# A refitted planner, a reordered opening and seven-product down matmuls from an earlier chunk, in a fused AFNO and GEGLU kernel

## The chip, the cores and the metric

The kernel runs on one core of one Trainium2 chip. Its time is the device time of one execution in microseconds (us); what counts is the median over the runs. The core has five engines that run side by side, each with its own queue in order: PE (TensorE, matmuls; its weight loads are listed as PEld), DVE (VectorE), ACT (ScalarE), POOL (GpSimd) and SP (SyncE, which here issues nearly all DMAs).

## The reference

A token-wise layer norm feeds two branches. Branch s is a Fourier transform over 8192 positions, a two-layer complex block MLP on the frequencies with a soft threshold, and the inverse transform. Branch g is a gated feed-forward network with 1792 hidden units. The output is the input plus their product.

```python
N, D, F = 8192, 448, 1792          # positions, channels, hidden units
xn = layernorm(x)
s = A(xn)      # rfft2 -> (x @ w1 + b1, relu) -> (@ w2 + b2) -> soft threshold 0.01 -> irfft2, 4 blocks of 112
g = silu((gelu(xn @ w_gate) * (xn @ w_up)) @ w_down)
out = x + s * g
```

All operands are float32. The kernel splits each into a high and a low float16 half, and makes one product from three matmuls: high with high, high with low, low with high.

## The kernel before

**The feed-forward network.** Positions are cut into 16 chunks of 512 tokens. The 14 slices of 128 hidden units are worked in two passes over all chunks: pass 0 has 8 slices, pass 1 has 6. A pass-0 result is stored to DRAM (`prt`) and fetched again in pass 1. Chunks 0 and 1 of pass 0 are computed plainly (`plain`, in `ffn`), while the weights still arrive. From chunk 2 on the up and gate products use Winograd's form of Strassen's scheme, seven products in place of eight (`unit`, with pairs of slices and halves of the tokens), on token factors that DMA transposes bring from DRAM (`xts` to `xta` and `xtb`).

**The down product of a chunk** has two forms. `down` makes 3 matmuls of 448 columns for each of 4 token tiles and each slice. `down2` uses seven products too: for each pair of slices 7 products, 2 halves and 3 matmuls of 224 columns, and once a 64-column filler. It needs sums of the hidden values (`sums` within `unit`; their halves go into the tiles `h`, `left` and, in pass 1, `wt`), and it adds the products up with `add2`, on ACT for the first part of a result and on DVE for the others. It also leaves a part of its work, the "tail", to be run inside the next chunk.

**The factored down weights.** `weights` first makes the combinations of the 8 near weight slices (`gu_comb`), then four times `factor0`, which fetches a pair of rows of the down weights, forms their seven factors and writes them to DRAM (`dsp`). When the fourth has been written, plus 3 us, `state["products"]` is set. `chunk` looks at it when it begins: at the first chunk that finds the flag and meets a condition on its number, it sets `seven` for good and starts `factors_in(0)`, 26 loads on SP that bring the factors into `dw`, `wt` and `left`.

**The other work.** Phase 1 runs beside the feed-forward network: `chunk1` normalises a chunk, writes its token factors (`xts`) and does the first stage of the transform, whose matmuls are called `bd<-xs,m`. `begin` does this for chunk 0 (`begin1` for chunk 1) together with the first weight slice; this is the opening. Phase 2 is the block MLP on the frequencies, phase 3 the inverse transform (`tiles3`) and the output.

**The order is planned when the program is built.** `Pace` is a small simulator of time. Every operation goes through `Engine`, whose call at L235 is the line of nearly every instruction in the profile. `Pace.start` asks when its engine and its operands are free, `Pace.cost` says how long it takes, and `Pace.issue` notes the end. The work is written as generators; whichever is due next in simulated time issues its instruction next, so the order of each engine's queue comes from the model. Side work asks with `calm`, which holds it back while its engine is busy or other work is due soon; `Either` gives an operation to whichever of two engines ends it first. The constants: `STEPS` gives corrections by stretch of time, `SLACK` a waiting time for PSUM banks, `T1` and `DT` the start of chunk 2's phase-1 work and the distance of the following ones, `END2` and `END3` the times over which the work of phases 2 and 3 is spread. The planner's times decide the order alone; on the chip the engines wait for one another with semaphores.

**The opening's weights.** `gu_loads` fetches the near slices 0 to 7 (`in_gu`, 512 KB each) into a ring `wst` of three slots, each large enough for a slice in its later form (`in_raw`, 17 columns of 128). `gu_block` and `gu_split` scale them into `wt`. Before the first matmul that counts, `keep` runs matmuls on ones.

Of the kernel before, what the change touches and what calls it, by code (L numbers as in the profile page):

```python
# [22 lines left out]
NG = 16  # L23
# [3 lines left out]
SLACK = 1.0  # L27
# [15 lines left out]
STEPS = ((0, 2.75, 0.05, 1), (100, 2.5, 0.15, 1.05), (175, 3, 0.2, 0.98), (250, 2.75, 0.05, 1), (325, 2.5, 0.05, 1), (400, 3.0, 0.1, 1.04), (475, 2.5, 0.05, 1), (550, 3.5, 0.05, 1), (700, 3.25, 0.3, 1), (775, 3.0, 0.3, 0.995), (850, 2.75, 0.05, 0.96), (925, 2.75, 0.05, 1.06), (1150, 2.5, 0.15, 0.995), (1450, 3, 0.1, 0.99), (1525, 2.75, 0.05, 1.02))  # L43
# [6 lines left out]
class Event:  # L50
    def __init__(self):
        self.done, self.waiting = False, []


class Pace:
# [4 lines left out]
    def __init__(self):  # L60
# [4 lines left out]
        self.late = False  # L65

# [72 lines left out]
    def ready(self, ap, write, engine):  # L139
        name, lo, hi = self.region(ap)  # L140
        return max((t + 0.12 for a, b, w, t, e in self.seen.get(name, ())
# [9 lines left out]
    def quiet(self, ap):  # L151
        return max((x[3] for x in self.seen.get(ap.tensor.name, ())), default=0.0)

    def start(self, e, out, ins):
        outs = [out] if out.space != bass.MemoryType.DRAM else []
        ins = [i for i in ins if i.space != bass.MemoryType.DRAM]
        return outs, ins, max([self.now, self.free.get(e, 0.0)] + [self.ready(i, False, e) for i in ins]
                              + [self.ready(o, True, e) for o in outs])

    def issue(self, e, op, out, ins, run):  # L160
        outs, ins, start = self.start(e, out, ins)
        if e == "SP" or op == "dma_start":
            size = (outs or ins)[0].nbytes()
            self.dma = max(self.dma, start) + size / (320e3 if start > 10.0 else 400e3)
            if start < 10.0:
                self.free[e] = start + 0.46
                end = self.dma + 0.9
            elif op == "dma_start_transpose":
                self.free[e] = start + 1.15 + size / 380e3
                end = max(self.free[e] + 2.6, self.dma + 1.5)  # L170
            else:
                self.free[e] = start + 0.5
                end = max(start + 2.2 + size / 240e3, self.dma + 1.5) + (self.step(start)[1] if outs and start > 100.0 else 0.0)
        else:
            end = start + self.cost(e, op, start, out, ins) * (1.0 if e == "PE" else self.step(start)[3])
# [2584 lines left out]
```

## Time and profile before

| | us |
|---|---|
| median of 3 runs (1759.02 to 1761.61) | 1759.36 |
| the profiled execution, own time | 1758.21 |
| its span, first to last instruction | 1756.4 |
| mean granted TensorE clock | 0.993 |

DMA moved 316.62 MB at a mean of 180 GB/s. The largest issues by count and size are the stores of token factors (`xts<-sx`, 32 of 480 KB), the loads of x and the raw weights (`wst<-in_raw`, 14 of 1088 KB). The factor loads appear as `dw<-dsp`, `wt<-dsp` and `left<-dsp`, the factor stores as `dsp<-wo`.

How to read the lines: a group is named out<-in by the program's tiles, with partitions x elements and type, then count, busy time and mean duration of one, then the idle time of the engine just before and what ended it. In a timeline a line has start, length, engine and operation; "x12" means that 12 alike were merged, and the bracket gives the idle time before it and who released it. PSUM banks are `bx`, `by` and `bd`. Matmul ends are modelled and matmuls overlap, so the price of one is read from the length of an unbroken run over its count.

### The profile page before, as it was taken

Reading aid. Unit: us, or ns where it says so; the run is one execution under the profiler, and the core shown is the slowest. Engines: PE = TensorE matmul, PEld = TensorE weight load, DVE = VectorE, ACT = ScalarE, POOL = GpSimd, SP = SyncE. Lnnn points to the kernel's source line nnn. Section 1 sums busy time; section 2 is a strip of 40 time slices with the busy share of each in tenths; the row PEclk is TensorE's granted clock in tenths of the full one; section 3 lists DMA queues with packets and bytes.
Section 4 is the critical chain, followed back from the end, with each engine's and each line's share of the span. In section 5 each row is a group of like instructions: output and inputs, shape, how many; then the busy total and the mean of one; then the engine's idle time right before and its main releaser. Section 6 shows DMA issues by size and latency. Waiting matters only on the chain.

```text
span 1756.4 us, 40962 instructions
## 1 busy us (share of the span) xinstructions
PE 1715.7 (98%) x15645; PEld 1435.9 (82%) x15645; DVE 1418.7 (81%) x2606; ACT 1113.9 (63%) x2279; POOL 751.5 (43%) x1083
## 2 busy tenths in 40 slices
PE   8998999999999999999999999999999999999997
PEld 4445677777777998999999989999899989889886
DVE  7898797777778877788887778888888887787787
ACT  6566676576676566778777666777676666333333
POOL 2277675566554564344333344432233432222222
PEclk9999999999999999999999999999999999999999
DMA  6428888887678653253445775445555545999996
GB/s 212 146 83 277 247 258 267 227 249 206 195 246 232 168 124 83 60 121 93 107 110 180 191 171 123 119 109 133 136 131 139 132 100 131 302 292 301 274 311 224
DMA packets 438308, 316.62 MB, mean 180 GB/s; under 512 B 305792, under 2 KB 409600, under 8 KB 436320
## 3 DMA queue, kind: packets, MB, share of 16 engines
q1 hardware_dynamic: 437824, 313.99, 63.6%
q8 instruction: 122, 2.00, 0.5%
q14 instruction: 74, 0.61, 0.1%
q10 hardware_dynamic: 288, 0.03, 0.0%
HBM read 137.93 MB, written 108.25 MB: 140 GB/s over the span
## 4 chain that ended last, share of the span: by engine, by line
PE 84%; DVE 7%; DMA 3%; ACT 3%; issue 2%; SPq 1%; POOL 1%; DVEq 0%; ACTq 0%; POOLq 0%
PE bd L235 34%; PE bx L235 29%; PE by L235 21%; DVE wt L235 1%; DVE u L235 1%; SPq L235 1%; DVE h L235 1%; DMA wst<-in_gu 1%; DMA prt<-th 1%; DVE va L235 1%; DMA xtb<-xts 1%; ACT h L235 1%; DVE o L235 0%; DMA vt<-va 0%; ACT o L235 0%
## 5 line engine op out<-in xcount | busy, mean ns | idle before, releaser
L235 PEld LDWEIGHTS <-wt 128*128 128x128 f16 x9142 | 887.2, 98 | 173.8 <-issue 19.4
L235 PE MATMUL bx<-xta,wt 128*128 128x256 f16 (+1 forms) x2819 | 355.5, 276 | 3.5 <-DMA xta<-xts 2.5
L235 PEld LDWEIGHTS <-h 128*128 128x128 f16 x2711 | 258.8, 98 | 73.5 <-DVE h L235 1.5
L235 PE MATMUL by<-xtb,wt 128*128 128x256 f16 x2080 | 255.7, 273 | 2.4 <-DVE by L235 1.3
L235 PE MATMUL bd<-dw,h 128*128 128x448 f16 (+1 forms) x1536 | 243.2, 306 | 0.0
L235 PE MATMUL bx<-xtb,wt 128*128 128x256 f16 x1248 | 153.2, 273 | 2.4 <-DVE v L235 2.3
L235 POOL TENSOR_TENSOR wt<-wt 128x256 f32<-128x256 f32 x81 | 63.0, 778 | 209.8 <-DVE wt L235 198.7
L235 PE MATMUL by<-xta,wt 128*128 128x256 f16 (+1 forms) x899 | 126.4, 285 | 2.7 <-ACT wt L235 1.9
L235 DVE TENSOR_TENSOR by<-bx,u 128x512 f32<-128x512 f32 x104 | 72.3, 695 | 43.4 <-PE bx L235 36.3
L235 ACT ACTIVATE u<-by,fc 128x512 f32<-128x512 f32 (+1 forms) x118 | 73.5, 635 | 47.9 <-PE by L235 47.0
L235 PE MATMUL bd<-dw,wt 128*128 128x224 f16 (+1 forms) x816 | 98.2, 264 | 3.6 <-DVE left L235 3.2
L235 PE MATMUL bx<-left,wt 128*128 128x256 f16 x816 | 100.0, 273 | 0.3 <-ACT by L235 0.3
L235 ACT COPY u<-by 128x512 f32<-128x512 f32 x104 | 60.7, 583 | 51.0 <-PE by L235 50.4
L235 ACT CAST h<-wt 128x512 f16<-128x512 f32 (+1 forms) x128 | 68.5, 536 | 36.1 <-DVE wt L235 29.1
L235 DVE TENSOR_TENSOR v<-bx,u 128x512 f32<-128x512 f32 x104 | 71.1, 684 | 16.1 <-PE bx L235 15.2
L235 DVE SCALAR_TENSOR_TENSOR left<-bd,ms,left 128x448 f32<-128x448 f32 x96 | 64.2, 678 | 22.5 <-PE bd L235 22.0
L235 ACT COPY by<-bx 128x512 f32<-128x512 f32 x104 | 60.1, 578 | 32.9 <-PE bx L235 32.6
L235 POOL TENSOR_TENSOR t<-h 112x256 f32<-112x256 f32 (+1 forms) x36 | 30.0, 832 | 114.3 <-ACT h L235 93.1
L235 PE MATMUL bd<-w2t,wn 113*128 113x112 f16 (+1 forms) x1152 | 78.1, 212 | 0.7 <-DVE wn L235 0.3
L235 PE MATMUL bd<-wt,h 128*128 128x224 f16 x603 | 72.2, 259 | 0.8 <-DVE h L235 0.7
L235 DVE SCALAR_TENSOR_TENSOR u<-by,fc,u 128x512 f32<-128x512 f32 (+1 forms) x86 | 55.4, 658 | 21.5 <-PE by L235 11.9
L235 PEld LDWEIGHTS <-wn 113*128 113x128 f16 (+1 forms) x1152 | 69.1, 97 | 3.8 <-POOL wn L235 0.6
(275 smaller groups left out, 3707.9 us busy)
## 6 DMA issues: line engine op xcount, KB each, us to landing
xts<-sx SPq DMA_DIRECT2D x32, 480.0 KB, 4.1
x<-in_x SPq DMA_DIRECT2D x17, 896.0 KB, 6.6
wst<-in_raw SPq DMA_DIRECT2D x14, 1088.0 KB, 7.0
t<-ysb SPq DMA_DIRECT2D x64, 224.0 KB, 3.5
prt<-th SPq DMA_DIRECT2D x64, 224.0 KB, 3.3
vt<-va SPq DMA_DIRECT2D x256, 56.0 KB, 2.1
left<-prt SPq DMA_DIRECT2D x64, 224.0 KB, 3.8
u<-t SPq DMA_DIRECT2D x32, 448.0 KB, 5.7
```

The source lines that it names most:

```text
L235: return self.pace.issue(self.name, kind, out, ins, lambda: fn(out, *args, **kw))
```

## The change

The change has three parts.

1. The planner's model is refitted. A result is seen by another engine after a delay that depends on the producer (`LATE`) instead of 0.12 us; an engine is free a little before its operation ends (`OVER`); any access to a PSUM bank waits for all others to it; DMAs get new rates, eight lanes and a lower rate for short runs; the costs of POOL and DVE are new; `SLACK`, `STEPS`, `T1`, `DT`, `END2` and `END3` get other values. No operation is added by this; the queues' order follows from it.
2. The opening is reordered. The near weight slices go into half-slots, six at a time instead of three; slices 6 and 7 wait until 0 and 1 have been read, and a whole slot is handed on for raw weights when both of its halves have been read. The number of matmuls on ones goes from 13 to 22. The maximum of the first weight slice is taken in two halves, and the normalisation and the casts of two token tiles stand between them. One low half moves from DVE to POOL and two go to DVE or POOL, whichever is planned to end first; the second copy of transposed tokens moves from ACT to DVE.
3. `chunk` asks for `i >= 2` instead of `i >= 9` before it goes over to seven down products.

The diff, cut to its core:

```diff
-SLACK = 1.0
+SLACK = 0.8
-STEPS = (...)
+STEPS = (...)
+LATE = {"PE": 0.2, "ACT": 0.04, "DVE": 0.04, "POOL": 0.05, "SP": 0.05}
+OVER = {"PE": 0.0, "ACT": 0.075, "DVE": 0.06, "POOL": 0.02}
...
     def ready(self, ap, write, engine):
         name, lo, hi = self.region(ap)
-        return max((t + 0.12 for a, b, w, t, e in self.seen.get(name, ())
+        write = write or ap.space == PSUM
+        return max((t + LATE[e] for a, b, w, t, e in self.seen.get(name, ())
                     if (write or w) and e != engine and a < hi and lo < b), default=0.0)
...
+            else:
+                turned = op == "dma_start_transpose"
+                slow = turned or min(self.run_of(a) for a in (out, ins[0])) < 512
+                self.dma = max(self.dma, start) + size / (210e3 if slow else 330e3)
+                self.free[e] = start + (1.0 + size / 305e3 if turned else 0.55)
+                end = max(self.dma + 1.7, self.free[e] + 2.6 * turned)
+            self.lanes = self.lanes[-7:] + [end]
         else:
+            n = start + self.cost(e, op, start, out, sb) * by
+            self.free[e] = n - OVER[e]
...
         if e == "POOL":
-            t = 0.7 if n < 8 and op == "tensor_tensor_pow" else 0.2 + 0.0023 * n
+            if n < 8:
+                t = 0.35 + 0.19 * n if op == "tensor_tensor_pow" else 0.25
+            elif sb < 2:
+                t = 0.18 + 0.00085 * n
+            else:
+                t = 0.18 + 0.0019 * n if out.dtype == F16 else 0.17 + 0.00217 * n
...
-    WS = ring(wp, [128, SL * 128], F32, "wst", 3)
+    raws = wp.tile([128, 3 * SL * 128], F32, name="raws")
+    whole = [raws[:, SL * 128 * k:SL * 128 * (k + 1)] for k in range(3)]
+    near = [whole[f // 2 % 3][:, 1024 * (f % 2):1024 * (f % 2) + 1024] for f in range(8)]
+    WS = Slots(pace, [])
...
-    T1, DT = 85.0, 34.5
+    T1, DT = 90.0, 34.0
...
     def gu_loads(fs, again):
         for f in fs:
-            t = yield from WS.get()
-            if f < 4 and not again:
-                yield 2.5 + 2.5 * f
+            if again:
+                t = yield from WS.get()
+            else:
+                t = near[f]
+                if f < 4:
+                    yield 2.5 + 2.5 * f
+                elif f > 5:
+                    yield ev("read", f - 6)
+                    yield pace.ready(t, True, None)
...
-            WS.put(t)
+            done("read", f)
+            if f % 2 and f > 1:
+                yield ev("read", f - 1)
+                WS.put(whole[f // 2 % 3])
...
-        if "products" in state and "seven" not in state and (p or i >= 9):
+        if "products" in state and "seven" not in state and (p or i >= 2):
             state["seven"] = True
             pace.spawn(later(lambda: factors_in(0)), pace.now + 2.0)
...
-    END1, END2, END3 = T1 + NG * DT + 12.0, 1450.0, 1730.0
+    END1, END2, END3 = T1 + NG * DT + 12.0, 1415.0, 1744.0
...
-        keep(13, 512)
+        keep(22, 512)
...
+        def widest(i):
+            V.tensor_reduce(mx[:, i:i + 1], t[:, 4 * i:4 * i + 4].rearrange("p k f -> p (k f)"), axis=AXIS.X, op=ALU.max,
+                            apply_absolute_value=True)
...
         root(0, 2)
-        V.tensor_reduce(mx, t[:, 0:8].rearrange("p (i k) f -> p i (k f)", i=2), axis=AXIS.X, op=ALU.max,
-                        apply_absolute_value=True)
+        widest(0)
         sums(1)
+        normal(0)
+        cast(0, 0, xss[0])
+        normal(2)
+        cast(0, 2, xss[1])
+        widest(1)
         squares(1)
...
+        low(G, 0, 0, xss[0])
...
-        S.copy(xT[:, :, 128:256], turned(banks[1]))
+        V.tensor_copy(xT[:, :, 128:256], turned(banks[1]))
...
-        low(V, 0, 1, xss[0])
+        low(B, 0, 1, xss[0])
...
-        low(V, 0, 3, xss[1])
-        WS.put(w)
+        low(B, 0, 3, xss[1])
+        done("read", 0)
```

112 lines of the change are left out of this document (63 added, 49 removed).

## Prediction

> **What bounds the kernel now.** I read the page first, then the busy time by stage, then the chain, then single stretches of the timeline.
>
> ```profile
> span 1756.4 us, 40962 instructions
> PE 1715.7 (98%) x15645; PEld 1435.9 (82%) x15645; DVE 1418.7 (81%) x2606; ACT 1113.9 (63%) x2279; POOL 751.5 (43%) x1083
> PE 84%; DVE 7%; DMA 3%; ACT 3%; issue 2%; SPq 1%; POOL 1%; DVEq 0%; ACTq 0%; POOLq 0%
> ...
> 0.00:62.00 62.00, 52.26 (x264) 25.36 (x265) 45.83 (x91) 38.85 (x92) 14.88 (x34) 0.90 0.59 196
> 62.00:273.00 211.00, 204.40 (x1288) 125.84 (x1287) 182.23 (x360) 141.80 (x280) 135.68 (x229) 0.99 0.69 209
> 273.00:550.00 277.00, 276.52 (x2103) 205.06 (x2102) 210.65 (x422) 184.38 (x357) 155.20 (x294) 1.00 0.81 231
> 550.00:1450.00 900.00, 888.34 (x9275) 818.49 (x9274) 736.68 (x1343) 625.23 (x1330) 365.12 (x444) 1.00 0.52 129
> 1450.00:1747.00 297.00, 294.18 (x2723) 261.17 (x2720) 238.27 (x384) 121.67 (x220) 80.63 (x83) 1.00 0.85 266
> 1747.00:1756.40 9.40, 0.00 (x0) 0.00 (x0) 5.00 (x11) 1.93 (x4) 0.00 (x0) 0.65 0.43 144
> ```
>
> The columns of a stage are its length, then busy time of PE, weight load, DVE, ACT and POOL, then the granted clock, the DMA share and GB/s. PE is idle for 9.7 us before 62, 6.6 us up to 273, 0.5 us up to 550, 11.7 us up to 1450, 2.8 us up to 1747, and for the last 9.4 us. Between 273 and 550 there is nothing to win but PE's own work: whatever takes matmul time out there shortens the kernel, as long as nothing else becomes late. The first 62 us is the other place, with a granted clock of 0.90. A busy PE could still be a slow one, so the price of one matmul has to come from long unbroken runs, which the chain in order of time gives (start, length, count):
>
> ```profile
> 312.56 17.03 PE bd L235 x90
> ...
> 648.75 6.90 PE bd L235 x72
> ...
> L235 PE MATMUL bd<-dw,h 128*128 128x448 f16 x768 | 152.4, 353 | 0.0
> ```
>
> The third row is from the groups by shape and gives a count only, 768 plain down matmuls (eight chunks of 96). The first is nearly all 448-column down matmuls, 17.03/90 = 0.189 us each; the second is 224-column down products, 6.90/72 = 0.0958 us each. Both scale with their columns; weight loads cost nothing visible.
>
> **Seven products: what a chunk saves.** A chunk of the first pass with plain down products has 4 token tiles x 8 slices x 3 = 96 matmuls of 448 columns: 96 x 0.189 = 18.1 us. With seven products it has 7 x 4 pairs x 2 halves x 3 = 168 of 224 columns, and one of 64: 168 x 0.0958 + 0.03 = 16.1 us. The saving is 2.0 us per chunk.
>
> The Trainium skill has a rule that speaks against this: "TensorE: Matmul & The Clock Gate", section "Back-to-back issue gap", gives a stream of weight load and matmul pairs some 81 ns per matmul at 128 columns and 131 ns at 512. Interpolated that is 94 and 123 ns at 224 and 448, so seven products would cost 168 x 94 - 96 x 123 ns = 4.0 us more per chunk, an estimate from that page. The two runs above contradict it (95.8 and 189 ns), and the measurement decides; I give it no chance.
>
> **Which chunks.** The diff says chunk 2, but the code also asks for the flag "products", which is set after the fourth write of factored down weights. These are SyncE's issues and the first matmuls of chunks 3, 4 and 9:
>
> ```profile
> 248.74 0.55 SPq L235 DMA_DIRECT2D dsp<-wo  x1
> ...
> 551.32 0.89 SPq L235 DMA_DIRECT2D dw<-dsp  x2
> 552.26 11.82 SPq L235 DMA_DIRECT2D wt<-dsp  x16
> 564.12 4.80 SPq L235 DMA_DIRECT2D left<-dsp  x8
> ...
> 215.68 1.47 PE L235 MATMUL bx<-xta,wt 128*128 128x256 f16 x12
> ...
> 272.97 1.47 PE L235 MATMUL bx<-xta,wt 128*128 128x256 f16 x12
> ...
> 550.00 1.47 PE L235 MATMUL bx<-xta,wt 128*128 128x256 f16 x12
> ```
>
> The fourth write is issued at 248.74, so the flag stands near 252 (the code adds 3 us). Chunk 3 starts at 215.68 and is too early by 36 us; chunk 4 starts at 272.97 with 20 us to spare. So seven products begin at chunk 4, not 2, and five chunks (4 to 8) change: 5 x 2.0 = **10.2 us** less PE work (2.03 before rounding).
>
> **What the switch moves.** The 26 loads that bring the factors now follow chunk 4's start instead of chunk 9's. On SyncE they took from 551.32 to 568.9, 17.6 us, and what queues behind them is the stores of the first stage, the stores of partial results and the next chunk's transposes. In the old place PE did not notice (0.5 us idle before 550, and none in the row of 593.5 to 642.9 below). At 273 the factors are first needed by the down products, which end a chunk of some 54 us, so the loads have over 30 us of cover. The DMA engines are fuller there, though. I charge nothing, which is the lower bound too, as no wait of PE goes away at chunk 9; the upper one is the whole 17.6 us.
>
> **What a chunk adds on the vector engines.** Chunk 10 already runs with seven products, with its neighbours in 593.5 to 642.9; its DVE groups show the new work. The last three rows are the plain chunk 7 (439.5 to 495.9):
>
> ```profile
> L235 DVE TENSOR_TENSOR h<-gl,h 128x256 f16<-128x256 f32 x6 | 3.6, 617 | 0.0
> L235 DVE TENSOR_TENSOR left<-u,left 128x512 f16<-128x512 f32 x4 | 3.6, 888 | 0.0
> L235 DVE TENSOR_TENSOR gl<-gl 128x256 f32<-128x256 f32 x4 | 2.1, 515 | 0.0
> L235 DVE TENSOR_TENSOR gl<-u,gl 128x256 f32<-128x256 f32 x4 | 1.9, 481 | 0.1
> L235 DVE TENSOR_TENSOR u<-gl,u 128x256 f32<-128x256 f32 x4 | 1.7, 425 | 0.1
> L235 DVE SCALAR_TENSOR_TENSOR th<-bd,ms,th 128x448 f32<-128x448 f32 x2 | 1.4, 683 | 1.7 <-PE bd L235 1.7
> L235 DVE TENSOR_TENSOR left<-gl,left 128x256 f16<-128x256 f32 x2 | 0.9, 440 | 0.0
> L235 DVE TENSOR_TENSOR u<-u 128x256 f32<-128x256 f32 x2 | 0.8, 413 | 0.0
> ...
> L235 DVE TENSOR_TENSOR h<-gl,h 128x512 f16<-128x512 f32 x3 | 2.1, 684 | 0.6 <-ACT h L235 0.6
> ...
> L235 DVE TENSOR_TENSOR sf<-sf,x 128x192 f32<-128x192 f32 x1 | 0.8, 775 | 0.0
> L235 DVE TENSOR_TENSOR sf<-x 128x192 f32<-128x192 f32 x2 | 0.7, 348 | 1.3 <-ACT x L235 1.3
> ```
>
> By the code each of the 4 pairs of slices has four sums (0.515 + 0.481 + 0.425 + 0.413 = 1.83 us), two low halves into h (1.23), one into left (0.44) and a wide one (0.89); a chunk adds three sums of partial results (2.05) and drops four wide low halves (2.74). That is 4 x 4.39 + 2.05 - 2.74 = 16.9 us more per chunk on DVE, or on POOL where the planner puts it. The stage from 273 to 550 gives DVE 210.65/5 = 42.1 us and POOL 31.0 us in chunks of 55.4 us. With seven products a chunk lasts 53.4 us: 11 us free on DVE, 22 us on POOL. The work fits if POOL takes a third of it, at up to twice the time, and the first stage's work for later chunks (which only asks when an engine is free) can slide. ACT, at 184.38/5 = 36.9 us a chunk, has 16 us free for three more casts per pair. I charge 1 us in all for waits that this adds; the lower bound is 0 (more vector work cannot help PE), the upper one is the slow rival below.
>
> **The opening.** Here is what PE and its suppliers wait for, PE first, then DVE and SyncE:
>
> ```profile
> 1.46 4.98 PE L235 MATMUL bx<-gl 128*128 128x512 f16 x13 [1.46 <-DVE gl L235]
> 8.74 0.22 PE L235 MATMUL bd<-ident,fx 128*2 128x128 bf16 x1 [2.31 <-DVE fx L235]
> 41.96 2.10 PE L235 MATMUL by<-xta,wt 128*128 128x512 f16 x7 [1.45 <-ACT wt L235]
> 57.95 0.17 PE L235 MATMUL bd<-ident,mxr 2*128 2x2 bf16 x1 [1.47 <-DVE mxr L235]
> 155.81 2.71 PE L235 MATMUL bx<-xta,wt 128*128 128x256 f16 x12 [2.46 <-DMA xta<-xts]
> ...
> 7.47 1.22 DVE L235 TENSOR_REDUCE fx<-wst 128x2 f32<-128x1024 f32 x1 [1.86 <-DMA wst<-in_gu]
> ...
> 30.84 14.98 SPq L235 DMA_DIRECT2D wst<-in_gu  x3
> ```
>
> Three things change. Nine more warm-up matmuls bridge the idle 2.31 us before 8.74. The reduction of 1.22 us is cut in two, with the normalisation between the halves, and DVE instead of ACT copies the second half of the transposed tokens: about 1 us (an estimate from that row) off the way to the first product. Before, tiles 5 to 7 were fetched one by one as slots came free, from 30.84 over 14.98 us; six half-size slots instead of three let tile 5 come at once, and waits such as the 1.45 us at 41.96 can go. Tiles 6 and 7 still wait, until 0 and 1 are read; behind them on SyncE stand the loads of the next tokens. Together that is at most the 8 us that PE idles between 1.5 and 62. But then PE meets chunk 2 sooner, and chunk 2's tokens come at 155.81, already 2.46 us late, out of a stretch where DVE is 86% busy (182.23 of 211). The wait costs more than itself: the 12 matmuls behind it took 2.71 us, where the same 12 took 1.47 at 215.68. So the opening's gain counts only as far as that arrival moves, and the change also starts chunk 2's work 5 us later (T1 85 to 90). Bounds: 8 us gained, 5 us lost. I take **2 us** gained, nearer to nothing, since the arrival row is the one that PE is held by.
>
> **The refitted planner and the end points.** Only the order moves, no PE work. Outside the opening 21.6 us of PE idle time is there to win or to double. Phase 2 gets 35 us less (END2 1450 to 1415) of some 800, so DVE's 82% in 550 to 1450 becomes about 86%; phase 3 gets more room. The tail of 9.4 us has the same steps. Bounds 7 us either way, a third of that idle time; I take 1 us gained.
>
> **The sum.** The profiled execution took 1758.2 us for its span of 1756.4, and the median of the runs, 1759.4, is 1.2 above it. 1758.2 - 10.2 + 1.0 - 2.0 - 1.0 = 1746.0; with the 1.2 the forecast is **1747 us**.
>
> **Rivals.**
>
> Opening paid in full: chunk 2's tokens come earlier too, since weights that arrive early let DVE use its 16 idle us before 62. For it: DVE is what feeds both. Against it: T1. 1759.4 - 10.2 + 1 - 8 - 1 = 1741 us.
>
> Chunk 2 late: T1's 5 us show in full and the opening gives nothing: 1759.4 - 10.2 + 1 + 5 - 1 = 1754 us. For it: that wait is there now.
>
> The change does less than it says: the flag slips by more than 20 us, to chunk 5, and four chunks change: 1759.4 - 8.1 + 1 - 2 - 1 = 1749 us. Against it: each of the four writes would have to come 5 us later.
>
> Slower: DVE becomes the bound in chunks 4 to 8. If 15 of the 16.9 us land on DVE, a chunk has 42.1 + 15 = 57 us of DVE work against the 55.4 us it lasts now, so five chunks lose 1.7 us each, 8.5 in all: 1768 us. It is slower from 13.3 us on DVE. For it: POOL can take less than its idle time suggests, because the two hold each other up: the same subtraction on DVE took 775 ns in one place and 348 in another of that window. Against it is this row of chunk 10, where all of the new work ran beside first-stage work and PE was busy for the whole 49.40 us:
>
> ```profile
> 593.50:642.90 49.40, 49.40 (x477) 45.95 (x475) 39.57 (x73) 33.31 (x68) 31.56 (x55) 1.00 0.53 128
> ```
>
> The Trainium skill ("SBUF — State Buffer", section "SBUF: two separate sides") says that a DVE operation with two SBUF inputs and a GpSimd operation lock each other out for a whole instruction. The 775 ns agree with that.
>
> **How the numbers follow.** The forecast has 0.69, the full opening 0.10, chunk 2 late 0.08, the late flag 0.06, the slow DVE 0.07. Within the forecast the opening can be 6 us better or 7 worse than taken and the planner's order 6 or 8; they will hardly err together, so 9 us to each side, 1738 to 1756, hold nine tenths of it, 0.62. Of the full opening, the late chunk 2 and the late flag, three quarters fall inside, 0.18 of 0.24; that makes 0.80. A measurement of this kernel tells 0.2%, 3.5 us, from no change: faster means below 1755.8. That is the forecast but for its upper edge (0.68), the full opening, the late flag and half of the late chunk 2: 0.88. No change has 0.06 (that edge, the other half of the late chunk 2 and the mild end of the slow case), slower 0.06.
>
> **What would show it.** Right: the factor loads (dw<-dsp) near 270, 224-column down matmuls from the chunk after them, five chunks some 2 us shorter, and PE still without waits between 270 and 550. The 768 plain down matmuls become 288. Wrong: PE waiting for left, h or wt behind DVE in those chunks; a wait for xta at chunk 2 longer than 2.46 us; dw<-dsp before 220 or after 320; more than 12 us of PE idle time in phase 2. If the clock still falls to half after 8.7 us, the nine warm-up matmuls did nothing.

## The result and the profile after

The change makes the kernel slower. Its median is 1784.12 us (1780.92 to 1785.37, 4 runs) against 1760.48 us for the kernel before on the same chip: a ratio of 1.0129, 95% interval 1.0108 to 1.015. The forecast was 1747 us with a range up to 1756, so it missed by 37 us and on the wrong side.

These are the span and the busy times of the changed kernel, its stages in the columns of the prediction, the plain down matmuls and the factor loads. All come from its profiled execution (1783.95 us). The line of the helper is now L275.

```profile
span 1781.8 us, 41978 instructions
PE 1717.7 (96%) x16031; PEld 1472.7 (83%) x16031; DVE 1497.2 (84%) x2682; ACT 1104.2 (62%) x2275; POOL 878.8 (49%) x1227
```

```profile
0.00:62.00 62.00, 58.07 (x313) 28.49 (x314) 52.23 (x105) 43.81 (x101) 25.47 (x46) 1.00 0.62 219
62.00:273.00 211.00, 202.10 (x1289) 126.48 (x1288) 183.05 (x360) 137.84 (x271) 116.14 (x205) 0.98 0.72 214
273.00:550.00 277.00, 259.22 (x2341) 227.56 (x2339) 251.07 (x445) 180.62 (x376) 201.43 (x315) 0.99 0.74 209
550.00:1450.00 900.00, 877.59 (x9087) 802.90 (x9086) 745.10 (x1345) 605.03 (x1279) 446.21 (x570) 1.00 0.52 129
1450.00:1747.00 297.00, 295.87 (x2790) 266.20 (x2789) 241.49 (x390) 124.48 (x227) 84.49 (x88) 1.00 0.89 259
1747.00:1781.80 34.80, 24.89 (x223) 21.03 (x220) 24.27 (x43) 12.38 (x22) 5.11 (x7) 0.95 0.44 151
```

```profile
L275 PE MATMUL bd<-dw,h 128*128 128x448 f16 x288 | 57.5, 353 | 0.4 <-ACT h L275 0.2 <-DVE h L275 0.2
```

```profile
270.60 1.15 SPq L275 DMA_DIRECT2D dw<-dsp  x2
271.80 12.29 SPq L275 DMA_DIRECT2D wt<-dsp  x16
284.14 3.75 SPq L275 DMA_DIRECT2D left<-dsp  x8
```

The switch took place exactly where the prediction put it: the factor loads begin at 270.60, and 288 plain down matmuls are left, three chunks of 96.

PE's idle time by stage, after against before, is 3.9 against 9.7 us up to 62, 8.9 against 6.6 up to 273, **17.8 against 0.5 up to 550**, 22.4 against 11.7 up to 1450 (more than the 12 us that the prediction named as a sign of being wrong), 1.1 against 2.8 up to 1747, and 9.9 against 9.4 in the rest. In all it is 64.1 against 40.7 us, 23.4 more, and PE's busy time rose by 2.0 where about 10 less was forecast. That rise is not work: the run with the old POOL price (below) has the same 16031 matmuls in 1706.5 us of busy PE. A matmul of 224 columns is shown as 259 ns long and the next can start after 96 ns, so the busy time also holds waits that are shorter than this overlap, and matmuls at a lower clock.

The stages are cut at fixed times, and the chunks shift against them. A cut at the first `bx<-xtb,wt` product of chunks 4 and 9 follows the work: at 285.82 and 560.48 us in the kernel before, at 279.44 and 571.15 in the changed one. These are the two rows, before first:

```profile
285.82:560.48 274.66, 274.18 (x2091) 203.91 (x2090) 208.93 (x419) 181.59 (x351) 152.59 (x289) 1.00 0.80 230
279.44:571.15 291.71, 271.94 (x2451) 239.03 (x2449) 265.19 (x484) 190.58 (x393) 207.78 (x328) 0.98 0.71 198
```

The changed kernel is 6.4 us ahead at chunk 4, takes 17.0 us longer for chunks 4 to 8, which were to get shorter, and 14.8 us longer from there to its end (1210.7 us against 1195.9). So there are two losses of like size: one in the chunks to which the seven products came, and one behind them. In the stage from 273 to 550 DVE went from 210.65 to 251.07 us and POOL from 155.20 to 201.43. The largest waits of PE there, each with its total, its count and the longest:

```profile
PE bx L275 <- DVE v L275: 5.1, 6, 2.6
PE bx L275 <- ACT by L275: 3.3, 3, 2.1
PE bd L275 <- ACT th L275: 2.6, 3, 1.3
PE bd L275 <- DVE h L275: 1.8, 1, 1.8
PE bd L275 <- DVE left L275: 1.4, 2, 0.9
```

Waits for `h` and `left` were the prediction's sign of being wrong; they came, but those for `v` and `by` are larger. The longest, 2.6 us for v, can be followed in the timelines of PE, DVE and POOL of the changed kernel (start, length, and for PE the idle time before):

```profile
403.26 2.72 PE L275 MATMUL bx<-xtb,wt 128*128 128x256 f16 x12 [2.61 <-DVE v L275]
```

```profile
398.48 0.41 DVE L275 TENSOR_TENSOR gl<-u,gl 128x256 f32<-128x256 f32 x1
398.92 2.96 DVE L275 TENSOR_TENSOR u<-gl,u 128x256 f32<-128x256 f32 x1
401.80 0.61 DVE L275 BATCH_NORM_STATS2 st<-x 128x6 f32<-128x448 f32 x1
402.45 0.18 DVE L275 BATCH_NORM_AGGREGATE st<-st 128x2 f32<-128x6 f32 x1
402.55 0.66 DVE L275 TENSOR_TENSOR v<-bx,u 128x512 f32<-128x512 f32 x1
```

```profile
397.91 1.29 POOL L275 TENSOR_TENSOR wst<-wst 64x128 f32<-64x128 f32 x1
399.17 0.58 POOL L275 TENSOR_TENSOR sf<-sf,x 128x192 f32<-128x192 f32 x1
399.72 1.87 POOL L275 TENSOR_TENSOR xs<-x,xs 128x896 f16<-128x896 f32 x1
```

`u<-gl,u` is one of the sums that seven products need; in chunk 10 of before it took 0.425 us. Here it starts at 398.92, while POOL is in an operation with two inputs, and ends at 401.88, only after POOL has finished three of them, the last at 401.59. `v`, which PE waits for, stands behind it in DVE's queue. Twelve matmuls after that wait took 2.72 us, where 1.47 is usual: the granted clock was 0.50 from 402.8 to 406.2. Two waits of 2.08 and 2.12 us in these chunks also ended in 3.4 us at 0.50, so such a wait costs more than itself.

### The profile page after: what moved, and what is told of

The parts are those of the page before. It is cut to its first block, busy times and chain, and to the rows that moved or that the text cites. A ratio compares the mean times of both kernels' runs of the same rounds, so it can differ in the third digit from the quotient of the medians.

```text
span 1781.8 us, 41978 instructions
## 1 busy us (share of the span) xinstructions
PE 1717.7 (96%) x16031; PEld 1472.7 (83%) x16031; DVE 1497.2 (84%) x2682; ACT 1104.2 (62%) x2275; POOL 878.8 (49%) x1227
## 5 line engine op out<-in xcount | busy, mean ns | idle before, releaser
L275 PEld LDWEIGHTS <-wt 128*128 128x128 f16 x9142 | 887.5, 98 | 192.3 <-issue 41.0
L275 PE MATMUL bx<-xta,wt 128*128 128x256 f16 (+1 forms) x2819 | 355.6, 277 | 13.3 <-ACT by L275 11.1
L275 PEld LDWEIGHTS <-h 128*128 128x128 f16 x2716 | 258.8, 98 | 41.6 <-DVE h L275 5.0
L275 PE MATMUL by<-xtb,wt 128*128 128x256 f16 x2080 | 258.3, 274 | 0.3 <-DVE by L275 0.3
L275 PE MATMUL bd<-dw,h 128*128 128x224 f16 (+1 forms) x1266 | 171.2, 281 | 4.6 <-ACT th L275 3.3
L275 PE MATMUL bx<-xtb,wt 128*128 128x256 f16 x1248 | 154.5, 274 | 12.3 <-DVE v L275 12.0
L275 POOL TENSOR_TENSOR wt<-wt 128x256 f32<-128x256 f32 x67 | 51.2, 764 | 184.1 <-DVE wt L275 174.1
L275 PE MATMUL by<-xta,wt 128*128 128x256 f16 (+1 forms) x899 | 124.0, 282 | 1.4 <-DVE u L275 1.3
L275 ACT ACTIVATE u<-by,fc 128x512 f32<-128x512 f32 (+1 forms) x118 | 73.6, 637 | 43.8 <-PE by L275 40.3
L275 PE MATMUL bd<-dw,wt 128*128 128x224 f16 (+1 forms) x816 | 99.2, 265 | 1.6 <-DVE left L275 1.2
L275 PE MATMUL bx<-left,wt 128*128 128x256 f16 x816 | 99.2, 273 | 0.0
L275 ACT CAST h<-wt 128x512 f16<-128x512 f32 (+1 forms) x128 | 68.6, 536 | 45.4 <-DVE wt L275 34.1
L275 DVE TENSOR_TENSOR by<-bx,u 128x512 f32<-128x512 f32 x104 | 72.0, 692 | 25.7 <-PE bx L275 22.9
L275 ACT COPY u<-by 128x512 f32<-128x512 f32 x104 | 60.6, 583 | 47.0 <-PE by L275 46.3
L275 DVE SCALAR_TENSOR_TENSOR left<-bd,ms,left 128x448 f32<-128x448 f32 x96 | 64.3, 679 | 27.4 <-PE bd L275 27.0
L275 PEld LDWEIGHTS <-left 128*128 128x128 f16 x864 | 82.5, 99 | 5.2 <-DVE left L275 1.9
L275 PE MATMUL bd<-wt,h 128*128 128x224 f16 x693 | 83.5, 259 | 2.9 <-DVE h L275 2.9
L275 PE MATMUL bd<-w2t,wn 113*128 113x112 f16 (+1 forms) x1152 | 79.0, 213 | 6.4 <-DVE bd L275 2.9
L275 PEld LDWEIGHTS <-wn 113*128 113x128 f16 (+1 forms) x1152 | 69.2, 97 | 11.1 <-issue 3.8
L275 DVE TENSOR_TENSOR v<-bx,u 128x512 f32<-128x512 f32 x104 | 70.9, 682 | 7.3 <-PE bx L275 6.9
L275 POOL CAST wn<-h 112x512 f16<-112x512 f32 (+1 forms) x43 | 32.9, 765 | 88.8 <-ACT h L275 88.8
L275 ACT COPY by<-bx 128x512 f32<-128x512 f32 x104 | 60.1, 578 | 22.6 <-PE bx L275 22.2
```

What stands on the lines that cost most here:

```text
L275: return self.pace.issue(self.name, kind, out, ins, lambda: fn(out, *args, **kw))
```

## The experiments

These theories were open. **E**: the added vector work fills DVE and POOL, which hold each other up, and PE waits. **F**: DVE's own work alone does it. **D**: the time lies in the order, and any other order than that of before costs. **A to C**, in the first runs: the vector work, the refitted planner and the opening, each blamed alone. Two kernels have no theory to test but a control: the PE work saved (**P**), and the warm-up matmuls (**G**). Where an expectation speaks of DVE's "excess", it can be read as the time that DVE's operations take beyond what they need undisturbed; the text goes by busy times instead.

### One part at a time

Two kernels take one part of the change alone, one takes the planner alone, one leaves out the seven products:

```diff
 seven only (of before)
-        if "products" in state and "seven" not in state and (p or i >= 9):
+        if "products" in state and "seven" not in state and (p or i >= 2):
 change without seven (of after)
-        if "products" in state and "seven" not in state and (p or i >= 2):
+        if "products" in state and "seven" not in state and (p or i >= 9):
 planner only: before with the new class Pace, its costs and constants
 opening only: before with the new gu_loads, begin and keep(22, 512)
```

> The kernel before, with nothing changed but the condition for seven down products (chunk 2 on in place of 9). Theory A, vector work: the sums of chunks 4 to 8 load DVE and POOL past what PE's time covers, whatever the planner, so this alone is slower than before by 8 to 25 us (1768 to 1785), with 10 us and more of PE idle time between 273 and 550 where there was 0.5. Theory B, the refitted planner's order: with the old order the 10 us of saved PE work show, 1747 to 1753, PE idle below 5 us there.

> The changed kernel with only the condition for seven down products put back to chunk 9. Theory A: 1750 to 1762, since the cause is gone, PE idle below 3 us between 273 and 550. Theory B: 1785 to 1795, since the saved PE work is gone and the bad order stays.

> The kernel before with the refitted planner alone (model, constants, start and end points), its opening and chunk 9 kept. Theory A: within 6 us of before, 1754 to 1766. Theory B: 1775 to 1795.

> The kernel before with the new opening alone (half-slots, 22 warm-up matmuls, halved maximum), old planner, chunk 9. Theories A and B both: 1752 to 1761, the first 62 us gain what they gained in the changed kernel (some 6 us of PE idle time) but chunk 2's input holds most of it back. If the opening is the cause (theory C): above 1770.

| kernel | us | ratio to before, 95% |
|---|---|---|
| seven only | 1796.47 | 1.0204 (1.0188 to 1.0219) |
| change without seven | 1772.11 | 1.0069 (1.0054 to 1.0084) |
| planner only | 1790.19 | 1.017 (1.0154 to 1.0185) |
| opening only | 1770.78 | 1.0052 (1.0035 to 1.0069) |

Every part alone is slower than no change (1760.05 us in these runs), and the three losses of 36, 30 and 11 us do not add up to the 24 of the whole. No theory that blames one part survives. With the seven products alone, chunks 4 to 8 took 274.7 us, as long as before: the saving was eaten there, and the 36 us lie behind. But each of these kernels also has a new order, so none of them measures its part by itself. The runs below therefore keep an order fixed where they can: the planner books an operation as before, and it is then left out of the queue, or one more is put into the queue that the planner knows nothing of.

### A new order with nothing else

```diff
 first neutral run (of before)
-    T1, DT = 85.0, 34.5
+    T1, DT = 85.0, 34.45
 second neutral run (of before)
-SLACK = 1.0
+SLACK = 0.98
 neutral run of the change
-    T1, DT = 90.0, 34.0
+    T1, DT = 90.0, 33.95
```

> The kernel before with one constant moved by a thousandth part of nothing to do with the change: the spacing of the phase-1 work, DT, from 34.5 to 34.45 us, so that the planner writes out another order of the same operations. Theory D (the order of before is one that fits the chip, and any other order costs): 1765 to 1790 us, with PE waits spread over stages the edit has no business in. Theory B (it is the refitted prices that give a bad order) and theory E (POOL gets more work and blocks DVE): 1757 to 1763 us, as neither prices nor work change.

> The kernel before with another constant that has nothing to do with the change moved a little: SLACK from 1.0 to 0.98 us, so that the planner writes out another order. Theory D (any order but the one that the constants were fitted to costs some 5 to 30 us): 1765 to 1785 us, with the waits in other places than in the first neutral run. If that first one (1772.13 us) was an accident: 1757 to 1763 us.

> The changed kernel with DT 33.95 in place of 34.0 us: another order of the same operations. Theory D: the time moves by more than 3 us from 1784.12, to anything between 1770 and 1800 us, as the order of the changed kernel is one draw among many. Theory E alone (only the amount of vector work and of POOL work counts): 1781 to 1787 us.

The first took 1772.13 us (ratio 1.0067, 1.0048 to 1.0085), the second 1766.08 (1.0039, 1.0024 to 1.0054), the neutral run of the change 1786.02 (1.0149, 1.0134 to 1.0164). Theory D is right for the kernel before: two constants that change no work cost 11 and 6 us. It is wrong for the changed kernel, whose time moved by 2 us only, as E expected. A fourth pair, further below, differs by 13.5 us. So a re-plan is worth 2 to 13.5 us here by itself, and no difference of that size between two plans can be put down to what was edited.

### The PE work at a fixed order

```diff
+            pace.ghost = p == 0 and 4 <= i < 9 and f in (1, 3, 5)
             T.matmul(ps, h(f, 0)[:, ts_], dw[1][:, f, :], start=False, stop=False)
+            pace.ghost = False
```

An operation that is issued while `ghost` is set is planned but not put into the queue.

> The kernel before in exactly its own order, but with 12 of the 96 down matmuls of each of chunks 4 to 8 left out of the queue (the high-by-low term of slices 1, 3 and 5): 60 matmuls of 0.189 us, 11.3 us of PE work, and a part of the product is missing. It is the size of the saving that the prediction counted, without another order and without vector work. If PE bounds the stage from 273 to 550 as predicted: 1747 to 1752 us. If the saving is swallowed by waits later (tokens, first-stage work, stores): 1756 to 1761 us.

With these 60 matmuls left out, so that a part of the product is missing, it took 1750.33 us, 10.7 less (ratio 0.9944, 0.9924 to 0.9963), for 11.3 us of matmuls. That step of the prediction holds: in the stage from 273 to 550, PE work that is not there shortens the kernel by itself, if nothing else is changed.

### Less vector work, and less POOL work, at the order of the change

```diff
 less vector work (of after): ghost set in chunks 5 to 8 around
             B.tensor_sub(a21, a11, a21)
             B.tensor_sub(a11, x, a11)
             B.tensor_sub(a12, a12, a11)
 and around two low halves into h
 copies for subtractions (of after), in Pace.issue
+        if e == "POOL" and op == "tensor_sub" and 290.0 <= start < 560.0 and out.tensor.name.startswith(("xs", "sx", "sf")):
+            return self.gpsimd.tensor_copy(out, ins[0])
```

> The changed kernel in exactly its own order, but in chunks 5 to 8 three of the four sums and the two low halves that each pair of slices adds are left out (about 2.65 us a pair, 10.6 us a chunk, 42 us of DVE or POOL time; the operands of the product are then wrong). Theory E (DVE and POOL block each other under the added work): PE's idle time from 273 to 550 falls from 17.8 us to below 9, and the time to 1770 to 1778 us. Theory D (the order itself is off): idle time there stays above 13, the time above 1780 us.

> The changed kernel in exactly its own order; POOL's subtractions in the first stage's tiles xs, sf and sx between 290 and 560 us (about 66 of 73 us) are copies of their first operand instead, about half as long and with one operand (the low halves of those chunks are then wrong). DVE keeps all of its work. Theory E: DVE's excess there falls from 44 us to below 32, PE's idle time from 17.8 to below 10 us, the time to 1766 to 1776 us. Theory F (DVE has too much work, whatever POOL does): idle time above 14 us, time above 1780 us.

Without some 42 us of vector work (the estimate above) the changed kernel takes 1761.9 us, 22 less. With copies in place of POOL's subtractions, and all of DVE's work kept, it takes 1765.2 us, 19 less. Both are below the range that E gave. The gain is where the cause is looked for: chunks 4 to 8 take 270.6 and 274.1 us instead of 291.7, and what follows takes as long as in the changed kernel to 2 us. Two rows for each kernel: the stage from 273 to 550, and `u<-gl,u` on DVE there (less vector work leaves most of these out, so it has the first row only).

```profile
273.00:550.00 277.00, 271.56 (x2512) 242.85 (x2510) 235.30 (x442) 193.12 (x403) 188.19 (x311) 1.00 0.78 217
```

```profile
273.00:550.00 277.00, 268.00 (x2474) 239.03 (x2473) 245.78 (x490) 190.49 (x395) 184.74 (x334) 1.00 0.76 215
```

```profile
L277 DVE TENSOR_TENSOR u<-gl,u 128x256 f32<-128x256 f32 x18 | 10.3, 571 | 1.4 <-POOL gl L277 0.9
```

```profile
L275 DVE TENSOR_TENSOR u<-gl,u 128x256 f32<-128x256 f32 x18 | 14.8, 823 | 1.8 <-POOL gl L275 1.3
```

The last row is that of the changed kernel. PE's idle time falls from 17.8 to 5.4 and 9.0 us. With POOL's subtractions gone, the same 18 sums on DVE take 571 ns instead of 823, though DVE does all of its own work. That speaks for E and against F, which expected over 14 us of idle time and over 1780 us: DVE lost time to POOL. The two savings of 22 and 19 us are not to be added; each relieves the same engine.

### The vector work at the order of before

The last four kernels put load on the engines of the kernel before, at its own order, on a spare tile that nothing reads. POOL gets 49 us of subtractions, or 46 us of copies; DVE gets subtractions; and one kernel has both kinds of subtractions. The diff is that of the last; in the kernels with POOL's load alone the POOL subtraction has 128 partitions instead of 64, and the copies come behind every third operation.

```diff
+        made = run()
+        if e in self.extra and 273.0 <= start < 550.0:
+            self.count[e] += 1
+            if self.count[e] % 4 == 0:
+                self.extra[e]()
+        return made
...
+    pace.extra["POOL"] = lambda: nc.gpsimd.tensor_sub(spare_g, spare_g, spare_g)
+    pace.extra["DVE"] = lambda: nc.vector.tensor_sub(spare_v, spare_v, spare_v)
```

> The kernel before in exactly its own order, with one more POOL subtraction (two operands, 128x240 float32, on a spare tile that nothing else reads) behind every fourth POOL operation that the planner places between 273 and 550 us: some 73 of about 0.7 us, about 50 us of POOL time, as much as the change added there. DVE gets no work. Theory E (a POOL operation with two operands holds DVE up): DVE's excess in that stage rises from 12 us to over 22, PE's idle time there from 0.5 to 4 to 10 us, the time is 1764 to 1772 us. Theory F (DVE simply has too much work of its own): POOL has 120 idle us there, so 1759 to 1763 us.

> The control of the run with the added subtractions: the same place, but copies with one operand (128x240 float16), one behind every third POOL operation, some 98 of about 0.5 us, again about 50 us of POOL time. Theory E in its strict form (only operations with two operands hold each other up): DVE's excess stays at 12 to 16 us and the time at 1759 to 1763 us. If POOL is merely late with its own queue, or any POOL work slows DVE, it comes out like the run with subtractions.

> The kernel before in exactly its own order, with one more DVE subtraction (two operands, 64x240 float32, on a spare tile that nothing else reads) behind every fourth DVE operation that the planner places between 273 and 550 us: some 105 of about 0.4 us, 40 us, so that DVE is as busy there as in the changed kernel (251 us). POOL gets nothing more. Theory F (DVE's own load is what makes PE wait): PE's idle time there from 0.5 to over 8 us, 1768 to 1778 us. Theory E (it takes DVE and POOL together): idle time below 4 us, 1759 to 1764 us.

> The kernel before in exactly its own order with both loads: the DVE subtractions of the run before this one and POOL subtractions behind every fourth POOL operation (some 73 of 0.7 us, 50 us), all on a spare tile that nothing else reads. It has the vector work of the change without its order and without its dependences. Theory E (both together): PE's idle time between 273 and 550 from 0.5 to 10 to 20 us, 1772 to 1785 us. If load alone is harmless even so, and it counts that PE waits for the added sums and that they stand elsewhere in the queue: idle time below 4 us, 1759 to 1764 us.

| load between 273 and 550 | us | ratio, 95% | DVE busy, whole kernel |
|---|---|---|---|
| none | 1760.46 | | 1418.7 |
| POOL subtractions | 1760.15 | 1.0001 (0.9991 to 1.0011) | 1433.9 |
| POOL copies | 1760.77 | 1.0003 (0.9993 to 1.0013) | 1425.6 |
| DVE subtractions | 1777.59 | 1.0094 (1.0077 to 1.0112) | 1478.8 |
| both kinds of subtractions | 1806.92 | 1.0252 (1.0231 to 1.0274) | 1503.8 |

The last two were measured beside a median of 1761.24 us of the kernel before. This is the cleanest table of the study, since order and dependences are the same in all five. POOL's load alone costs nothing, DVE's 16 us, and both 46 us, nearly three times as much. F, DVE's own work, was right for both runs with one load: 1760.15 us, and 1777.59 us with 11.2 us of PE idle time in the stage. E as it was stated failed in both. But F has no place for the run with both, where the POOL load that is harmless alone adds 29 us to DVE's 16; E expected that it takes both, and forecast 1772 to 1785, too little. So neither holds as stated. The rows of the stage show why. They are those of POOL subtractions, DVE subtractions and both:

```profile
273.00:550.00 277.00, 276.88 (x2105) 205.14 (x2103) 226.17 (x423) 184.53 (x358) 207.03 (x367) 1.00 0.81 231
```

```profile
L240 DVE TENSOR_TENSOR h<-u,h 128x512 f16<-128x512 f32 x18 | 16.5, 918 | 1.0 <-ACT h L240 0.9
```

```profile
273.00:550.00 277.00, 265.77 (x2022) 197.82 (x2020) 250.93 (x465) 176.87 (x347) 160.50 (x286) 0.99 0.76 220
```

```profile
L626 DVE TENSOR_TENSOR spare<-spare 64x240 f32<-64x240 f32 x90 | 49.2, 547 | 2.5
```

```profile
273.00:550.00 277.00, 252.92 (x1862) 183.89 (x1861) 250.89 (x433) 161.12 (x315) 186.11 (x330) 0.98 0.72 209
```

```profile
L628 DVE TENSOR_TENSOR spare<-spare 64x240 f32<-64x240 f32 x83 | 48.5, 584 | 2.3
```

And the same group of low halves in the kernel before, without load:

```profile
L235 DVE TENSOR_TENSOR h<-u,h 128x512 f16<-128x512 f32 x18 | 13.9, 775 | 0.9 <-ACT h L235 0.9
```

POOL's 49.2 us of subtractions made those 18 operations slower, 918 ns against 775, and raised DVE's busy time in the stage by 15.5 us, from 210.65 to 226.17, but PE stayed busy (0.1 us idle): DVE had room. In the two other kernels DVE stands at 250.93 and 250.89 us of 277, where the first was laid out to come near 251, and in the changed kernel at 251.07. With POOL's load added to DVE's, DVE's busy time in the stage did not rise any further; PE fell behind instead. So about 251 of 277 us, 91%, is what DVE reaches in this stage when PE waits for it. It is no sharp edge. With 235 and 246 us in the two kernels above, PE was idle for 5 and 9 us; and in the kernel with the seven products alone, DVE was busy for 92% of 99 us, with PE idle for 0.4:

```profile
456.00:555.00 99.00, 98.62 (x925) 89.42 (x923) 91.00 (x157) 66.79 (x137) 69.17 (x115) 1.00 0.69 190
```

Taken as a rough measure, 251 leaves 40 us above 210.65. DVE's busy time over the whole kernel rose by 60.1 us under its own load, 20 more than the room, and the time by 16; with both loads it rose by 85.1, 45 more than the room, and the time by 46. With POOL's subtractions it rose by 15.2, within the room, and the time not at all. One account fits all four loads: **what counts is DVE's time including what POOL makes it wait, and only the part beyond some 40 us costs.** The 40 us are an estimate that fits these runs, not a limit that one of them shows, and a little of the load falls behind 550.

### What the planner gives to POOL

```diff
 old POOL price (of after)
-                t = 0.18 + 0.0019 * n if out.dtype == F16 else 0.17 + 0.00217 * n
+            t = 0.7 if n < 8 and op == "tensor_tensor_pow" else 0.2 + 0.0023 * n
```

The other two are this kernel with `i >= 9`, and with DT 33.95.

> The changed kernel with the planner's old price for POOL (0.2 us + 0.0023 us an element) instead of the refitted, cheaper one; all else of the change stays. Theory E: less is given to POOL (busy 760 to 810 us instead of 878.8), DVE is blocked less (excess between 273 and 550 from 48.7 to below 38 us), 1765 to 1778 us. Theory D: another order that was not fitted to these constants, POOL less busy, but the time 1780 to 1800 us.

> The changed kernel with the old POOL price (1767.09 us) and the seven products from chunk 9 on as before, not from chunk 4. It says what the five chunks are worth where POOL is given less. If they pay the 10 us of PE work: 1774 to 1780 us. If they are worth nothing: 1764 to 1770 us. If they still cost what they cost under the refitted price (12 us): 1752 to 1758 us. A new order adds its own scatter to each (theory D).

> The changed kernel with the old POOL price (1767.09 us) and DT 33.95 in place of 34.0 us: another order of the same operations. Theory D: the time moves by more than 3 us, to anything between 1755 and 1785 us. Theory E alone: 1764 to 1770 us.

They took 1767.09 us (ratio 1.0034, 1.0024 to 1.0045), 1762.45 (1.0011, 1.0001 to 1.002) and 1780.63 (1.0119, 1.0102 to 1.0136). The first alone would look like proof that the refitted POOL price costs 17 us. The third takes that back: the same prices with another DT lie 13.5 us higher, as theory D expected and E did not. Nor did POOL do less in the critical stage, as this row of the first shows (200.79 us against 201.43 in the changed kernel):

```profile
273.00:550.00 277.00, 265.17 (x2446) 236.43 (x2446) 245.34 (x441) 187.59 (x389) 200.79 (x318) 1.00 0.75 210
```

So what the refitted price is worth stays open. Under either price the five chunks did not pay: with the old one 1767.09 and 1780.63 with them against 1762.45 without, with the refitted one 1784.12 against 1772.11, and at the planner of before 1796.47 against 1760.05. Each pair has the scatter of its two orders in it. Chunks 4 to 8 by themselves took 277.6 and 287.9 us with seven products against 280.6 without, 291.7 against 282.1, and 274.7 against 274.7. None is 10 us shorter; one is 3 us shorter, two are 7 and 10 us longer, one is the same.

### The warm-up alone

```diff
         keep(13, 512)
+        for _ in range(9):
+            nc.tensor.matmul(first[0][:, 0:512], ones[:, 0:128], ones[:, 0:512], start=True, stop=True)
```

> The kernel before in exactly its own order with nine more matmuls on ones at the start and nothing else. The prediction said that they bridge the idle 2.31 us before 8.74 and keep the clock up. Granted clock from 8 to 16 us 0.9 or more instead of about 0.57. Theory G (the opening is paced by DVE and the loads, so a faster PE only waits longer): time within 1 us of before, 1759 to 1762 us. If the clock counts there: 1755 to 1758 us.

Nine matmuls on ones at the fixed order of before gave 1757.82 us (ratio 0.9987, 0.9975 to 1.0), with these rows of its timeline, its first stage and the time from 8 to 16 us:

```profile
6.53 2.11 PE L2475 MATMUL bx<-gl 128*128 128x512 f16 x9
8.64 0.22 PE L235 MATMUL bd<-ident,fx 128*2 128x128 bf16 x1
```

```profile
0.00:62.00 62.00, 53.78 (x276) 26.04 (x277) 47.09 (x94) 40.25 (x93) 16.36 (x35) 0.93 0.59 196
8.00:16.00 8.00, 6.97 (x51) 3.97 (x50) 7.34 (x19) 6.68 (x16) 2.91 (x7) 1.00 0.66 270
```

They do bridge the gap before `fx`, and the granted clock rises as expected, to 1.00 from 0.57 between 8 and 16 us and from 0.90 to 0.93 in the first 62. The interval reaches no change, so a gain is not shown; if there is one it is a few us. Of the kernels that compute all of the reference, none had a lower median than this one.

## Why the prediction was wrong, point by point

**The price of seven products** stands: in the changed kernel three runs of 12 such products start at 501.63, 502.78 and 503.93 us, 0.0958 us for each product as taken. That PE work left out shortens the kernel stands too: 11.3 us less at a fixed order gave 10.7. The five chunks and the moment of the switch came out exactly.

**The failed step** is "I charge 1 us in all for waits that this adds", with what led to it, "11 us free on DVE, 22 us on POOL. The work fits if POOL takes a third of it". With the saving and this 1 us, chunks 4 to 8 were to become 9.2 us shorter. They became 17.0 us longer, 26 us off, and 7.4 of these are there without the seven products as well (282.1 us against 274.7, another plan). What is left, some 19 us, is what the two runs at the order of the change show: the waits cost 19 to 22 us. The condition was met: against the change without seven products DVE was busy for 50.6 us more (1497.2 against 1446.6) and POOL for 29.2 (878.8 against 849.6), so POOL took about a third (DVE's figure holds its waits for POOL). It did not fit all the same. Room was counted up to 100% of a chunk. By the rough measure of 251 in 277 us a chunk of 55.4 us holds 50.2 us of DVE work, so the room over 42.1 us was 8 us, or 6 in a chunk of 53.4, not 11 (an estimate). And POOL's third was not free: 49 us of POOL subtractions cost DVE 15.5 us.

**The slower rival** had the right mechanism and the right place, at a chance of 0.07. It put the turning point at 13.3 us on DVE per chunk and the price at 8.5 us in all. With a turning point near 8 us, the bound was reached by what a chunk adds, even with POOL's share taken off. What argued it down was the row of chunk 10, where all the new work ran without a wait of PE. But DVE and POOL together were busy for 39.57 + 31.56 = 71.1 us there, including the new work, against 42.1 + 31.0 = 73.1 us in a chunk of the stage without it. Chunk 10 had less other work, by about as much as the seven products bring. By the us it was a little fuller than the plain stage (71.1 of 49.4 us against 73.1 of 55.4), but the changed stage has 251.07 + 201.43 us in 277, more than either. Both figures stood in the prediction, and were not set beside each other.

The Trainium skill's rule, "SBUF — State Buffer", section "SBUF: two separate sides", that a DVE operation with two inputs in SBUF and a GpSimd operation that reads SBUF exclude each other for a whole instruction, agrees with the 775 ns that became 918 under POOL's subtractions, and with the 0.425 us sum that took 2.96 us.

**The opening** did better than forecast at its place: PE idles 5.8 us less up to 62, the clock there is 1.00 instead of 0.90, and chunk 2's first product comes at 147.12 in place of 155.81, so 8.7 us earlier, against 2 forecast and 8 as the bound:

```profile
147.12 1.47 PE L275 MATMUL bx<-xta,wt 128*128 128x256 f16 x12
...
153.04 1.79 PE L275 MATMUL bx<-xta,wt 128*128 128x256 f16 x10 [3.36 <-ACT by L275]
```

The tokens' arrival no longer holds PE, so "chunk 2 late" was wrong; a wait of 3.36 us, for ACT and `by`, stands a little behind it. Of the 8.7 us, 6.4 are left at chunk 4 in the changed kernel. With the opening alone nothing is left there (288.4 us against 285.8), and that kernel takes 1770.78 us: a new order can eat this gain.

**"The refitted planner and the end points", "I take 1 us gained"**, also failed: the change without the seven products is 12 us slower than before, although its opening gains, and the planner alone 30. The bound of 7 us either way was too narrow. Two neutral constants that cost 11 and 6 us show that a good part of it needs no fault in the refit. How the 12 us divide between the refit and any new order was not settled.

**The sum** then reads, by stretch of the work (us in the profiled executions, cut as above):

| kernel | up to chunk 4 | chunks 4 to 8 | from chunk 9 on |
|---|---|---|---|
| before | 285.8 | 274.7 | 1195.9 |
| the change | 279.4 | 291.7 | 1210.7 |
| seven only | 286.9 | 274.7 | 1233.6 |
| change without seven | 279.9 | 282.1 | 1208.6 |
| less vector work | 280.1 | 270.6 | 1209.8 |
| copies for subtractions | 280.3 | 274.1 | 1209.0 |
| first neutral run | 288.3 | 278.2 | 1206.5 |
| second neutral run | 287.4 | 276.4 | 1200.2 |
| DVE subtractions | 287.8 | 294.3 | 1197.2 |
| both kinds of subtractions | 289.4 | 319.2 | 1199.3 |

The forecast of 1747 us missed by 26 us in chunks 4 to 8 and by some 16 behind them, and the opening gave some 4 back. The larger part of the first is shown at a fixed order to be the vector work. The second is there without the seven products too (12.7 us longer than before): all thirteen kernels with another order than that of before are 4.3 to 37.7 us longer from chunk 9 on, and the six that load or relieve engines at that order 0.9 to 4.2 us. So it goes with the new order; what in an order costs it, no run shows.

## What to carry to other kernels

An engine's room ends before 100%, and at no sharp edge: look for the busy shares at which its consumer begins to wait, and compare the load of a stretch that is held up as proof with that of the stretch in question before trusting it. Work given to POOL is paid for on DVE as well, here at no cost while DVE had room, and in full once it had none (25 us more on DVE and 29 us more of time, both loads against DVE's alone), so two loads that are cheap alone can be dear together. Where an order is planned by a model, compare with a neutral re-plan first, measure an edit at a fixed order, and cut the time where the work begins and ends, not at fixed times.

## What the hardware showed that was not expected

A waiting DVE operation need not get its turn after the POOL operation that it waits for: in one place that the trace shows, the 0.425 us sum sat through 0.58 and 1.87 us of POOL operations that began after it, for 2.96 us in all.

POOL copies with one operand hold DVE up too, at about half the rate of subtractions: 46 us of them raised DVE's busy time in the stage by 8.2 us, from 210.65 to 218.85, as this row of that kernel shows, and 49.2 us of subtractions by 15.5. The strict form of E, that only operations with two operands count, is not borne out. The section of the Trainium skill named above speaks of any GpSimd operation that reads SBUF, and with that this row agrees.

```profile
273.00:550.00 277.00, 277.00 (x2109) 205.56 (x2108) 218.85 (x423) 183.97 (x355) 199.82 (x391) 1.00 0.81 233
```
